# Last eight tiles of the second linear layer: all products copied out of PSUM by ScalarE, all residuals added by TensorE, and a new order table

## The chip, the core and the metric

The kernel runs on one core of a Trainium2 chip. A core has a matrix engine (TensorE, PE in the profile; its weight loads are PEld), a vector engine (VectorE, DVE), an engine for functions of one operand (ScalarE, ACT), a general engine (GpSimd, POOL) and SyncE (SP), whose queue issues nearly all transfers (DMA). Each engine runs its own list of instructions in order and waits on semaphores. Matrix products are written to PSUM, an on-chip memory of accumulators, and have to be read from there by VectorE or ScalarE. SBUF is the on-chip memory of the operands. The metric is device microseconds (us) of one execution; less is better.

## The reference, cut to what matters

There are 2048 tokens of 512 channels and four residual layers, A, B, A, B:

```python
x = x + _A_ref(_layernorm(x), ...)      # memory-augmented attention, 32 heads of 16, 4 segments of 512 tokens
x = x + _B_ref(_layernorm(x), ...)      # linear attention with a learned feature map
x = x + _A_ref(_layernorm(x), ...)      # the same weights again
x = x + _B_ref(_layernorm(x), ...)
```

Layer B is the one that the change touches:

```python
phi_q = concat([softmax(pq), softmax(-pq)])          # 32 features per head and token
phi_k = concat([softmax(pk), softmax(-pk)])
kv  = einsum('bhsf,bhsd->bhfd', phi_k, v);  z = einsum('bhsf->bhf', phi_k)
num = einsum('bhqf,bhfd->bhqd', phi_q, kv)           # the numerators
den = einsum('bhqf,bhf->bhq', phi_q, z) + 1e-06
return (num / den) @ wo                              # then added to x
```

`kv` and `z` sum over all tokens. So no query of a B layer can be finished before the last key of it has been seen, and in the second B layer nothing but its queries is left to do after that.

## The kernel before, in words

The tokens lie in SBUF as 16 tiles of 128 tokens, `X[:, t, :]`. The host code builds a graph of operations for both layer pairs (L = 0 and L = 1): `ln` normalises a tile and transposes it, `a_proj` makes queries, keys and values of a segment of four tiles, `a_att` does the attention of two tiles, `out_proj` multiplies by the output weights and adds the result to `X`, `b_keys` does the key side of B, and `b_query` the query side for a block `c` of four tiles, 4c to 4c+3.

The order of the work is not written in the loops. `ORDER` is a packed table with three parts: the order of all operations, the engine of each (some may run on either ScalarE or VectorE), and the buffer of each tile of the pools. `place` reads it, and `emit` writes each engine's list and the semaphore waits that the data and the reuse of buffers ask for. An operation that takes a buffer waits for all readers of the buffer's last content. PSUM has four such buffers, `pD0` to `pD3`, of 1024 columns each; the pool `p1` of small SBUF tiles has ten, `p2` of larger ones twenty-two. A wait at the head of an engine's list holds up everything behind it on that engine, and SP's queue is such a list too.

The start. The tokens and all weights are loaded by large transfers (512 KB for four tiles of tokens or for one weight matrix), most of them on SP's queue. Tiles 0 to 3 are transposed on PE, and tiles 4 to 7, the second segment, by SP: `xn` (line 597, VectorE) writes a normalised tile and a DMA transpose (line 364) puts it into a buffer of `pX`. The first projection of the second segment needs all four of these transposes. The large loads and the transposes share the queue, so a load that SP issues first is ahead of the transpose.

The end. After the last keys, `b_query` runs for the four blocks of L = 1, in the order 0, 2, 1, 3. For each block, PE makes the query features and their sums (`Zq`), ScalarE takes the exponentials, and a short chain of small ScalarE (`zln`) and VectorE (`zs`) steps makes the 64 weights `AB` per token; line 360 or 359 first copies the sums out of PSUM in blocks 1, 2 and 3 (`Zev`). Then for each tile:

- PE writes the numerators, 128 x 1024 in f32, to a PSUM buffer (`N`).
- They are multiplied by the weights. For a tile in `COPIED`, ScalarE copies them to SBUF as bf16 (`Nev`, line 351) and VectorE multiplies in SBUF (line 1084). For another tile VectorE multiplies straight from PSUM (line 1087).
- VectorE adds the two halves (`nadd`, line 1090). For tiles 0 and 15 PE does it (line 894), and the sum is copied out of PSUM (`ote`).
- SP transposes the result (`otr`, line 364). PE multiplies by the output weights (line 341), for two tiles at a time, and for tiles 14 and 15 one at a time.
- The residual: for tiles in `RES_PE`, PE adds `X` as one more product with the identity matrix, and the sum is copied to `X` by ScalarE (line 359) or VectorE (line 360). For the others, VectorE adds the PSUM buffer to `X` (line 925).
- SP stores the rows of `X` (line 368).

The two branches for the numerators are these:

```python
if (L, t) in COPIED:
    self.act(lambda Ns=Ns: Ns.t[:], lambda N=N: N.t[:], ACT.Copy, 1024, [N], [Ns], label="Nev")
    v(lambda e, ...: e.tensor_tensor(shape(Tm.t[:]), shape(Ns.t[:]), w(), ALU.mult), 600, ...)
else:
    v(lambda e, ...: e.tensor_tensor(shape(Tm.t[:]), shape(N.t[:]), w(), ALU.mult), 1131, ...)
```

Of the kernel before, what the change touches and what calls it, by code (L numbers as in the profile page):

```python
# [297 lines left out]
class Kernel:  # L298
# [147 lines left out]
    def T(self, pool, cls):  # L446
        return Tile(pool, cls)
# [726 lines left out]
c-rlH1GHt=vUXwmSZ&+3ZQHhO+qP}nM$$~$HiJge2)fh%+WRDV$-T+D_l@zt@ngKT_gQnzxvFYbeO2>YYmR-ALkdU(bs;q*fqGCM8bCv61dX8yG=*l+99lq2Xa%jI4  # L1174
YY-J&>lKKN9Y8dp$l|{_>chNK|)9h3KBs|NCpU1p)3F}RD+^W4vK*T0s$IgKx~i@1d$L37OF#Wr~xIQJmiI%kPq@h0jK~ap%#>af>03(K_#dSb)XxRhVD=X3PWZ19;
!eO=n1``2#kbuFbYOPdYA^|U;^}prO*dPz#DiA26Dk2$O)<7G2DfBkQTmy_wX(J08ii^+=r)-9iBlBcmXfr0gQzVkQ*k#c*qLRVGMi)51}u-f&w@gmqC9R0Lx($yoM
oI5C_3F7>*-wJB-B5PzXoi8YqlgU=s9$fv^LHz)BblA@Cz~#p%!yyJ07s0b5}*{DP}tEzE>Zm=VHZD0~fJ@CZWTJJ<=k;ByFu0LXz^@F!RTIWa3{!=GU&YRrzqushC
!9%yh51n~!$4XYqAWCM%Eu^8sTT$m4YV^7SBQy@R~!jJF^Oobvi7KcG+EQ;fBK74}VumDQnI+z83nV=-@h9tNLRzOnhi+dp%B6dNC<FOx3z~nd@*I)`9gKKdWPR0Q^
1?R#-U|bJ`De)UzjU#9gOvK*UA4gIjTnyi0W+;tia07gY-{VG@gzIoWl*a=w2-jl;+<*g7^9uwz2!?;aH~11QBfZ6`m<OieaUeq8h&8bm#>J{w4a;IVjEC{@M-0F$@
CuKCz&bbsD`7>PiPf<(*1#$ljKiol*2Q|b1w-&NI0>n-6xK)L2ABYc(^lMuoA4Zj;yXMKU%+<Uj7#tg%%U$L63@a<_%nXMKum-QF@pC&I39u%FdZAB#E;0d6lc>;+=  # L1180
cUS2QI=!I3E||9Gr`daRDyGCK!eh7=%sH@oRjKvv4=g#%WZTmSII&i7T)ORiYWR95d2%nn`nLE@h$sPK<jn2JXdRZibnuIkv!-7|E^i2(-ZvW^Rj7+zv<4XevwjC_j
~>0u)A@s32{o;uKDWs67^?Q&55g6{9FTM2AVzX^5bhs4xOzLMq&ct*`?s+Cckp5N)K&RE5e@NjiX$RDl9$FvY?%co0uuAjP1Q_!)kVhwv~4Q4BtUr*Ive#ZnXpW8-=
{hhu0geSzty8l|VIG>%GB8OlJRd=v#&ry4Y#T2d>@fXyi*wxBdPfhJN~JcgMtiX^AQwlsv=QB#^iQ)wtQqq<a&CR2TCO>L+F)uzVOgw{|UYDn{_5ly1Clo`)sdaOx?
j)JByu|0L5j&vH2V<5+cT9lPK(R{j&3uqB7p&NJsFXAO!NQ>zv-p1s#ly=ZEN<rIbIqjsBbQm1PBuim@3-90xT1hdvGaaEWbQibNQCdY^DVS#S9KMVr`3inUqj(E_P
O)eo#ina`72{BRN<?v~8}*^S6a`u6B7{&Z4rj&paVs65{j`Vn(lI(n$7wg6pa(dbAL2>6hhum;pQY1Og3r({n!zQx9G{}cn2^fzBTP-_C;^?Pew3XnaSkrVmAN>_=A
j&ib8=$pPCckU^`s;em*dfD8pbm@5vQVAT!AZcVt$Upc?5rj@i_^np|3F+SLbSc8In>c72%>>maFnaeu4*i5?A3e{1nG?DK5>2cmk)TUi1ZhNzbqb51^Xdo7QtKUdS
7G5%1^xe1HpZZXU~Xc`8riaa@q+aUssb11T9@g2J4Tlkx?c!bkZSFXknDkuFg@zDc*J887F_JfEBMU~a%GcmX%$AzY8^^D<t`OSu(i;C0-Z5AzYO#VdIgU#8W3g%WT
b&d8fN6W8VYw1pdUBW}ShxeY&{w%ml<aZ_&3pL0r1#hLjbo#MyTNHi9==_*~LJ9L+>Qx;CnDYyf7<W8KLbJ0o8O?fCi-++z$8E2#Hw3RQwJ*v(5xHISFSg?j~&?deK
X*nzBphxtC&hl|S#|^|bKEVw|7v9NTc{}gor?i82b189}&+uLj5c{~acus+$f~Y9=a5<5a(s4HK#(nubf5H8@KM&wE{3Uni9^8|A@mCZfz9uWmi)R!moQM)J#6ZqV-
_W<zn_p0v2p2Eu6@`d6B2;K$#4Q*mVu{!ySOkff;yW5H>WB+Gi2LwucujG|_Y_ZD<hr7sxWvswebHQ8<|}-QuW~g(qJ@y+4Y8;$9&jb`kcDU|DvP(IL=(|QT!U*IUt  # L1190
EXVe4X#`UB1UPMGetblo5~k9W@nC_&rq-Wkpr-1C0`+MQhPX)Do>kVo_T><)7$BYA4!@&LW9ODw2s`D4|FsK2d4`e1jiz8j)UP5XnVKkxKkbX~hTXA~J~-BBMwrGK(
zYBV`rYM0Sxt+~=E|Lv$76#1;6O$BPM~hj_+c@kG&6Jm+utD)bRAd4%XIMv52wEx+P!qPr*|a*AFemw3&+#rIrNbP%~k9+6iR5^p%4$S(?r!s0tFB8rM)Vvv|Bn#g{
lzZfE#$^l}q7$b&?vEnT^lkfQ*H<ts&4?IOo7L&w}{8UU6)5Q!iQ*;z@pr9x&W{GEFwpb$Oh@bdp{=iGcbMcj!E9Qx1V!l`|R)_^+p;#$aiI2QaeB$+DyZD6{iN#{I
SR>Yo4Pui3u~BRmD9(tpVuxrU&xtR@VX<2r5qm^SxkYRh+r&|^SL_$(#ZIwH>=OsXA#qR~7stex;)1v+E{P86vgoKDidM3<ydqAB&&5e`N<0!*#WnGnxFhb0)8d}EE
^de?@}_toZj1ZkmguB9tH<JN@j`qno``S6OYus)7T<~Q#T(H^eiTn-TiIT=lRt=GL<jjy{wO-ix1y7LC!WjB^1b*Zy2!8O*HX$h3S?XLja0I${7H0^D1R1Ceh^xID_
_f3@`ZdUhs*9VK=zO$<ae^C43uM}kz*yvAlXiRFRf(RU%rv;)c`qCj*{bKupBRid@DobXgNXllD%c9MAcnc)m3#--Bg&IC@0A{GF--$?_`7=DBsI?GE&BuQ8JB8E0f
3=GO0`_)5`=hrpzFJkO^fnnOvrj8D&c8R1Za}r}|O$Qa{N=GL}pw6U)gmwfrD6$=Gs`{8?s}ALVovtg^^KDyy8K2CIUyiYz3v$q<!W7M6WvZ`D_>lmUv>FEW?>Bv;8
m)ko!&*<}v7TCS0cWM37kgjy@B%E7Xq93t<l1bV0pQ;TIkHB45M4^%?^wW=;N=^FC3`bK5e{nZ^cKoya9)jd^I7L%ZYlvGRPQn^g7lQrcOIa^MZbL3n(P0o|k<#IVt
<&}A42{~VulIvwHSzCsyr)s!TDxKD9gi5cUsfu#EnxIz58FGP~DUF(`O3LDLq?)BhsWNh*oFyyC%JPMZr@vJZD!zWMzEY7Yk$$8K>zC@WdZnJIhbpnoprcei8AH8R-
>JQ_h|Z`>>U}ba&ZSG~q&m0WAY-cia-y1~hNz(`g-)sC=#4V2F0QZ3Ec%8lp|k2MvbHWQ>*)AuliVzC%48~=zACTD{IY<YtVXM0>U(ut&Q@FHHhD`<QQ37eom_91Q&  # L1200
nDFN9NHvbSj-jr`2_3PJKYWQ>pcPHBD`iWo0>8PbOD8Wm=U^tyKxsFY1#Tqh9K<iu5bZI=}uw<<mRlI8{KeQw8;p>WzA<=BVm=u98~l8X7d}pVjyJC-qU4)=F#rLCs
UUWO|iBB~*#jdX+-OQYqC2HD7I1TU176bSh<aY_&|y({FScJzt-fWpz1SUVkBr>I%A;J|g3&#44_;FO#S*<srFMZByG-O<hYLl^0}1U0E;Em2_3TSXa}_)dICpEmFt
iXEL?gp$^JSYLmJocgsD}>7*)+DlaR@%qpHLqyzK<9jF)T&*dFiMX%C#WsqL1?#b19jb5vl>ScPlUZI!hx_YBtsT=AIdc9t!>*@Nsk#3+*%M&tEpOib*ad}EEQJeH;
eOKSpP4sQuKsMG5Wix$WH`T#9N*|VuWQdM$n(G!iRL9UU^$N98h3UpJmOdjd%F8lb-_do{1D(LU*N=5w^+f-mU+XODJN;I_(^*wLl}*jmv-E8JRL{``)lEHD-_p-?Z
uPT%t_!J{=7au9$1?TRL)}0XR(aJHokO+M=j3J;q0h?LdX;LZ9_erN11Zfz`9goKizsCt$vo=5T&?n{oa#p%*L>8i^iMjTiEUczIHs5?s@muRs*&2N^Q!<8Xg=w0^)
3zOfY#<0y<7Lx2emOr^ikbQ_tu?t7u{B)X{WpDZo0khpvmM?9d&lqT_4hibzfao9oN;=F?~XB(<k)~-A7kf{q%OdQ#Vn2^$OEe?a?dEe!Wj8HO<r@o!Ioyo%Cn=bIs
<Iek_ZtnyRrnt#_$4YN_h4lNoD*%wRoGCo#chfOck>PG}OD;ktwhGb41k8KrBeA$q7Tsgj!%CennMk-C&RqgR=;I@IhitIbXmWn!47rkP1)mYI|$!n8G`^*McBmsMZ
r)FzE7qe`o^X1Ten+MDL)ifU)Z=oY4<>0rj{PUf0gVy>&DrktvvuByxWhN`8m=-TRmX=6H@)~2!PYPy*&=74!<nwZ_{pxI;gnmwwOS!Y_BL#n(=XN1|Sx|<$mz1d|B
tNx~**=+`x`evMNVA7j==Dt~Ej;Mp`kU4BJn8hZeIiM=49A=+6X119v=D0ay_M7eItQoHxnxkfonV^rVwWg8DWG3pIW|FR?zSI}=MV;AfFdNM|v&n2VL(O?J%p5Vj&
# [61 lines left out]
```

## Time and profile before

| | |
|---|---|
| median of 3 runs | 477.54 us (476.16 to 478.46) |
| the profiled execution, its own time | 477.2 us |
| its span, first to last instruction | 475.5 us |
| PE busy | 450.5 us (95%) |
| ACT busy | 424.1 us (89%) |
| DVE busy | 418.5 us (88%) |
| POOL busy | 54.7 us (12%) |
| granted TensorE clock, mean | 0.996 |

The profile has a page (busy time by engine, the span in 40 slices of 11.9 us, the chain of work that ended last, groups of like instructions) and views of the trace behind it: the timeline of one engine, the chain in order of time, busy time by windows, and the transfers of a window with the time from issue to landing. In a timeline a row gives start, duration, engine, line, operation, tiles, and in brackets the idle time before it with what seems to have ended it. The duration of a row includes its start-up, which overlaps the end of the row before it: from one start to the next on a busy engine, a row costs some 0.1 us less than its duration.

### The profile page before, as it was taken

To read this page: it belongs to the slowest core of one execution; us is meant where nothing else is said; L and a number is where in the kernel's file an instruction comes from. 1 tells how busy PE (TensorE), PEld (TensorE's weight loads), DVE (VectorE), ACT (ScalarE), POOL (GpSimd) and SP (SyncE) were. 2 spreads that over 40 slices of the span, in tenths; PEclk is the share of its full clock that TensorE was granted. 3 is DMA by queue.
4 is the path that set the end of the run, shared out by engine and by line. 5 is a ranking of instruction groups with operands and counts; after the bars stand their busy time and mean duration, and the time that the engine had idled before them with its cause. 6 is when DMAs were issued, how large, how long until landed. Compare 5 with 4: busy or idle time off the path is not lost.

```text
span 475.5 us, 25072 instructions
## 1 busy us (share of the span) xinstructions
PE 450.5 (95%) x11583; PEld 296.2 (62%) x11583; DVE 418.5 (88%) x812; ACT 424.1 (89%) x567; POOL 54.7 (12%) x139
## 2 busy tenths in 40 slices
PE   9979999999999999999999999999999999999885
PEld 4447665767667676565555666666666667666542
DVE  6969999999699888987999998998897887898994
ACT  3869999999999998579999999999999999786961
POOL 2301112001011101100220041110020020110000
PEclk9989999999999999999999999999999999999999
DMA  9941292352423132100133334343104404100256
GB/s 233 248 84 39 42 127 56 76 66 48 69 51 60 25 42 33 24 1 4 37 80 70 81 47 72 69 71 59 26 5 81 61 4 70 37 12 3 55 81 204
DMA packets 89388, 30.36 MB, mean 64 GB/s; under 512 B 75954, under 2 KB 89282, under 8 KB 89282
## 3 DMA queue, kind: packets, MB, share of 16 engines
q1 hardware_dynamic: 88450, 28.20, 32.0%
q8 instruction: 91, 1.49, 1.3%
q10 hardware_dynamic: 800, 0.52, 0.4%
q14 instruction: 15, 0.12, 0.1%
q0 software_dynamic: 32, 0.02, 0.0%
HBM read 6.31 MB, written 2.10 MB: 18 GB/s over the span
## 4 chain that ended last, share of the span: by engine, by line
PE 64%; ACT 21%; DVE 12%; issue 2%; POOL 1%; DVEq 0%
PE D L341 40%; PE D L326 21%; ACT p L351 10%; ACT pF L351 7%; ACT pE L351 3%; DVE p L1087 2%; PE D L662 2%; DVE p L1084 2%; DVE X L925 1%; DVE p L360 1%; DVE p L1090 1%; DVE pT L1007 1%; DVE pK L360 1%; PE D L378 1%; DVE pV L360 1%
## 5 line engine op out<-in xcount | busy, mean ns | idle before, releaser
L351 ACT ACTIVATE p<-D 128x1024 bf16<-128x1024 f32 (+1 forms) x220 | 217.5, 1018 | 12.8 <-PE D L341 7.8
L351 ACT ACTIVATE pF<-D 128x896 bf16<-128x896 f32 x128 | 115.7, 927 | 5.1 <-PE D L326 4.5
L326 PE MATMUL D<-pK,pQ 64*128 64x256 bf16 (+3 forms) x1536 | 113.7, 243 | 4.3 <-ACT pF L351 1.9
L326 PEld LDWEIGHTS D<-pK,pQ 64*128 64x128 bf16 x1536 | 55.4, 94 | 40.8 <-ACT p L351 5.2
L326 PE MATMUL D<-pV,pF 64*128 64x34 bf16 x1024 | 76.5, 176 | 1.6 <-issue 0.8
L326 PE MATMUL D<-pW,pF 64*128 64x34 bf16 x1024 | 73.9, 176 | 0.0
L326 PEld LDWEIGHTS D<-pV,pF 64*128 64x128 bf16 x1024 | 57.2, 93 | 5.8 <-ACT pF L351 2.1
L588 POOL TENSOR_SCALAR rstd<-mv 128x1 f32<-128x1 f32 x60 | 15.0, 256 | 359.7 <-DVE mv L581 359.5
L326 PEld LDWEIGHTS D<-pW,pF 64*128 64x128 bf16 x1024 | 53.5, 93 | 1.4
L326 PE MATMUL D<-pV,p 64*128 64x34 bf16 x1024 | 53.1, 176 | 0.6 <-issue 0.2
L351 ACT ACTIVATE pE<-D 128x768 bf16<-128x768 f32 x64 | 52.1, 821 | 1.5 <-PE D L326 0.9
L326 PE MATMUL D<-pW,p 64*128 64x34 bf16 x1024 | 51.7, 176 | 0.0
L326 PEld LDWEIGHTS D<-pV,p 64*128 64x128 bf16 x1024 | 47.0, 93 | 3.3 <-issue 0.7
L326 PEld LDWEIGHTS D<-pW,p 64*128 64x128 bf16 x1024 | 45.4, 93 | 1.6
L326 PE MATMUL D<-tri,two 64*128 64x128 bf16 (+1 forms) x384 | 46.2, 234 | 0.2 <-issue 0.2
L326 PE MATMUL D<-pV,pE 64*128 64x34 bf16 x512 | 45.0, 175 | 0.0
L580 DVE BATCH_NORM_STATS2 stats<-X 128x6 f32<-128x512 bf16 x64 | 43.2, 682 | 2.0 <-DMA X<-in_A_x_dram 1.7
L326 PE MATMUL D<-pW,pE 64*128 64x34 bf16 x512 | 43.2, 175 | 0.3 <-issue 0.3
L341 PE MATMUL D<-pX,WA_k 64*128 64x512 bf16 x256 | 37.3, 383 | 2.8 <-ACT pF L351 2.6
L972 DVE TENSOR_REDUCE pS<-p 128x64 f32<-128x1024 bf16 (+1 forms) x36 | 38.5, 1090 | 1.4 <-ACT p L351 1.2
L925 DVE TENSOR_TENSOR X<-X,D 128x1024 bf16<-128x1024 bf16 (+1 forms) x29 | 32.0, 1107 | 8.4 <-PE D L341 8.3
L341 PE MATMUL D<-pX,WA_q 64*128 64x512 bf16 x256 | 37.6, 384 | 0.6 <-DVE pV L360 0.5
(132 smaller groups left out, 992.3 us busy)
## 6 DMA issues: line engine op xcount, KB each, us to landing
pW<-pV SPq DMA_DIRECT2D x16, 136.0 KB, 3.6
out_dram<-X SPq DMA_DIRECT2D x7, 256.0 KB, 4.2
X<-in_A_x_dram SPq DMA_DIRECT2D x3, 512.0 KB, 5.7
pX<-in_B_wqkv_dram SPq DMA_DIRECT2D x3, 512.0 KB, 5.0
p<-p SPq DMA_TRANSPOSE x76, 2.7
pX<-p SPq DMA_TRANSPOSE x54, 3.3
WA_k<-in_A_wk_dram SPq DMA_DIRECT2D x2, 256.0 KB, 6.8
WB_o<-in_B_wo_dram SPq DMA_DIRECT2D x8, 64.0 KB, 3.6
```

Source lines behind the costliest of these rows:

```text
L326: ins = e.matmul(out_ap, lhsT, rhs, start=st, stop=sp, tile_position=(basep(lhsT), basep(out_ap)))
L341: ins = e.matmul(out_ap, lhsT[64 * hf:64 * hf + 64], rhs[64 * hf:64 * hf + 64], start=k == 0 and i == 0, stop=k == 1 and i == len(lists[hf ...
L351: return self.g.op({"act": (dur, lambda e: e.activation(out_ap(), in_ap(), func, scale=scale))}, reads, writes, opens, label=label)
L360: "dve": ((340 if fast else n / 0.96 + 65), lambda e: e.tensor_copy(out_ap(), in_ap()))}
L378: ins = e.transpose(pb()[:, k * 128:(k + 1) * 128], src()[:, k * 128:(k + 1) * 128], self.ident[:])
L580: v(lambda e: e.bn_stats(self.stats[:, t, :], self.X[:, t, :]), 602, [R("X", t)], [R("st", t)], label="bn")
L588: v(lambda e: e.tensor_scalar(rs, self.mv[:, t, 1:2], LN_EPS, None, op0=ALU.add), 170, [R("mv", t)], [R("rstd", t)], eng="pool", label="rstd")
L662: ins = e.matmul(D.t[c0:, r0 * 8:r0 * 8 + n], r[:, c0:], ones(r, n), start=True, stop=True, tile_position=(r0, c0))
L925: self.v(lambda e: e.tensor_tensor(X(), X(), src(), ALU.add), 65 + 512 * n / 0.96, pr + xr, xr, label="res")
L972: fn = lambda e, sgn=sgn, eo=eo, Z=Z, n=n: e.tensor_reduce(Z.t[:, 0:64 * n].rearrange("p (k s h) -> p k s h", k=n, s=2)[:, :, sgn, :], eo( ...
L1084: v(lambda e, Ns=Ns, Tm=Tm, w=w, shape=shape: e.tensor_tensor(shape(Tm.t[:]), shape(Ns.t[:]), w(), ALU.mult), 600, [Ns, AB[0], AB[1]], [Tm ...
L1087: v(lambda e, N=N, Tm=Tm, w=w, shape=shape: e.tensor_tensor(shape(Tm.t[:]), shape(N.t[:]), w(), ALU.mult), 1131, [N, AB[0], AB[1]], [Tm], ...
```

## The change

Two sets grow and the table is replaced:

```diff
-RES_PE = {(0, t) for t in (2, 3, 6, 7)} | {(1, t) for t in (2, 3, 6, 7, 10, 11, 14, 15)}
+RES_PE = {(0, t) for t in (2, 3, 6, 7)} | {(1, t) for t in (2, 3, 6, 7, 8, 9, 10, 11, 12, 13, 14, 15)}
-COPIED = {(0, t) for t in range(16)} | {(1, t) for t in range(1, 16, 2)}
+COPIED = {(0, t) for t in range(16)} | {(1, t) for t in range(1, 16, 2)} | {(1, t) for t in range(8, 16)}
 ORDER = """
-c-rlH1GHt=vUXwmSZ&+3ZQHhO+qP}nM$$~$HiJge2)fh%+WRDV$-T+D_l@zt@ngKT_gQnzxvFYbeO2>YYmR-ALkdU(bs;q*fqGCM8bCv61dX8yG=*l+99lq2Xa%jI4
...
+c-rlH1(Y2}vSmPWGl`j*nVFfHnVFfHnVFfH8Ei4wV%Y*)GDx;q*01+ko^N|*c4qhNKMUtqt1GMWMMg&4xN*CxTME)ZU8o23p#e06Mi3toKtf0YNue<`f#eVmQb1E^2
...
```

In L = 1, tiles 8, 10, 12 and 14 go over to the copied branch (four more ScalarE copies, and four multiplies that read SBUF in place of four that read PSUM), and the pairs (8, 9) and (12, 13) over to the residual on PE (eight more matrix products with the identity, and two copies to `X` in place of two additions).

The new table has 2761 operations where the old had 2757. It gives another order, other buffers, and another engine to 21 of the operations that can run on either. Those of them that bear on a count are, in the order of the work:

- at the start, the normalisation `xn` of tile 3 goes from VectorE to ScalarE, and one copy of a weight matrix (`perm`, 512 columns) from VectorE to ScalarE
- in the third and fourth segment of L = 0 two projection copies of 1024 columns change places, one to each engine
- in L = 1 a projection copy of 512 columns goes to VectorE and a copy of 272 columns to ScalarE
- at the end, the copy of the sums of block 1 (`Zev`) and the copy after the addition on PE of tile 0 (`ote`) go from ScalarE to VectorE; the residual copies of tile 14 and of (6, 7) go to VectorE, and those of tile 15, (8, 9) and (12, 13) are on ScalarE

In SP's list at the start, the old table has, after the loads of the first weights, this order: tokens 8 to 11, transpose of tile 7, tokens 12 to 15, transpose of tile 5, weights for B's keys, transpose of tile 4, weights for B's values, transpose of tile 6. The new one has: tokens 8 to 11, tokens 12 to 15, transposes of tiles 6 and 7, weights for B's keys, transposes of tiles 5 and 4, the two swaps of the values (line 736), weights for B's values. Ahead of these stand the same first loads in both; in the new table the A values' weights have moved up, ahead of the second half of the A queries' weights and of the A output weights. In VectorE's list `xn` of tile 6, the last of the four in the old order, comes first, and that of tile 4 last.

At the end, the old list of SP has all stores behind all transposes; the new one has the store of (2, 3) between the transposes of tiles 8 and 4. Four of the additions `nadd` wait in the new table for a transpose as well, the last reader of the `p1` buffer that they write (tile 9 for the transpose of 2, tile 4 for 10, tile 6 for 9, tile 13 for 4).

More of the change, by code (lines that the diff above doesn't have):

```diff
@@ L1178 @@
[L1178 to L1189, printed above, removed]
@@ new lines @@
+O|&C=G?72t0?E@GabdAK*v$1%86NkO+Q;N01ACg;$UR?!jYt0@<Mq^n_lJ4o1Q#NDrf78uW%fkQ44hZWsq+;5Cee4Dbf}!UPx(BVZ{M!UDJq2IC+oj0JHBZiA6H3b#
+X6=nn(oDLjDh;2}(cA+QPh!EzW317HWNhKaBOhT|F-ft#T#Zh>yt5j){@$bmB;C(eX*uoYgwTX=yhVF|2)p)d==;CuK6e#2}q8Fs=h2!+#d0#3n6$c9<)9c0I>I27M
+QcN~U2P~$3Gjq||Z2Y7}V!D4aDjm0n*=EJ<0ABRC6oB}<uC>FstI2@+JY(VUVC2%g3#E$^@2|i(8OoC&vACAM_Fdp|nQXGwIVJ|FzWH=u(K>+>+$#DWY9D|)P1+KxA
+_!8H{LYM<@u?w!n0XTvt;w0>i8=yaqq&~P2O5-9}hY`FO%HVpOjQe2&PQe4P5zFI19E26HEGC9P3}R%$gTR;;p5s)Uh6di@FZe6ILV=ninb@%9AJFl81VW19AF(FJ#
@@ new lines @@
+d25+tKtldht)7X9*4{@6DwjRtd2FX4%Wsh7>skU9@fQ8SQ!)GTnxblxEU8>eI#mtOK=-TKrp1nFQ60#L0m|M3SXndh8T(;FdWapdH52R;&z;e^YIJ}qYH2rV&Fvx!e
+EZTERYC)!bm&>VYmgS<3}%*pK&-X!{s=OcHlJHinD1tHNsig7@J^1oQ;ccCyt`sxC<-NVjN8?u`tb`6<CRi&`iomb0`zdrKZ>n6XQN;jx8{R_uyV^iLJ2>W~O|Up9)
+YI6{NCMh@!9@6{T?6M8#+`2|7fFiMcI?atv;V?J<I4Vid(fNs9JiOlXB2Fb>AX;<O(JQ3;Bq4Rio2(_lJ?0UVP9+0r3Aftq5_VcbXoREA1Zc`8Zga2-{l3UnSz(HN>
+m>nR;orS$X#j-?COoLW$II)X>B24$d=cnSp{!<uv&$I*C7gDt5QWx%vJfimJmN{5*+h|b_qa1_RpGvk+N=pweIA=HlQ(iECXL#ZA$rDiml>Qe)nM2)F7wWc-HhU(Bf
@@ L1233 @@
+qk=hB1SLIh)=N1SkjL4pIrNPA7;1cnGt&5S}v9O>&Tk8R}Z83^?f@cPGS3h{}iCpcjqVXY@ao~Y7)0Ay;S$N
 """
```

96 lines of the change are left out of this document (50 added, 46 removed).

## The prediction

> **What bounds the kernel now.** First the busy shares on the page, by slice.
>
> ```profile
> PE   9979999999999999999999999999999999999885
> DVE  6969999999699888987999998998897887898994
> ACT  3869999999999998579999999999999999786961
> PEclk9989999999999999999999999999999999999999
> ```
>
> One slice is 11.9 us. From the fifth to the 37th PE hardly rests, and ACT only in slices 16 and 17, so time can be won only where all three engines rest at once: in the third slice, where the granted clock falls too, and in the last four. Next, PE's timeline and the windows around the third slice:
>
> ```profile
> 23.52 0.22 PE L326 MATMUL D<-tri,two 64*128 64x128 bf16 x2
> 26.39 1.04 PE L341 MATMUL D<-pX,WA_k 64*128 64x512 bf16 x8 [2.65 <-ACT pF L351]
> 27.25 0.37 PE L326 MATMUL D<-pK,pQ 64*128 64x256 bf16 x4
> 27.44 0.23 PE L326 MATMUL D<-tri,two 64*128 64x128 bf16 x2
> 27.50 1.70 PE L341 MATMUL D<-pX,WA_k 64*128 64x512 bf16 x8
> ...
> 28.00:29.40 1.40, 1.40 (x11) 0.73 (x9) 0.17 (x1) 0.63 (x1) 0.00 (x0) 0.50 0.60 141
> 29.40:31.00 1.60, 1.60 (x11) 0.71 (x8) 1.60 (x5) 1.34 (x2) 0.00 (x0) 0.50 0.41 82
> ```
>
> PE stands still for 2.65 us before the first projection of the second segment, and then the granted clock (third figure from the end) is 0.50 until 31. The timeline names an ACT row as what ended the gap, but the chain in order of time has
>
> ```profile
> 24.46 0.95 ACT pF L351
> 25.41 0.98 issue
> 26.39 1.04 PE D L341 x8
> ```
>
> ACT had been done for 0.98 us, so it was another wait. The code has it: this projection needs the transposes of tiles 4 to 7. In the transfers of the window 19.6 to 21, the last of these is
>
> ```profile
> pX<-p SPq DMA_TRANSPOSE x1, 6.5
> ```
>
> issued at 19.64, so it lands at 26.14, right before PE goes on. The same view gives 4.3, 5.0 and 4.8 us for the other three, issued at 13.28, 15.65 and 17.77. ACT in turn idles 2.32, 1.03, 0.36 and 0.62 us up to 33.2, 4.3 us in all, waiting for PE.
>
> Last, the end, in VectorE's timeline:
>
> ```profile
> 441.13 1.22 DVE L1087 TENSOR_TENSOR p<-D,pS 128x1024 bf16<-128x1024 f32 x1
> 442.27 0.28 DVE L1059 TENSOR_TENSOR pS<-pS,p 128x128 f32<-128x128 f32 x1
> 442.47 0.42 DVE L1090 TENSOR_TENSOR p<-p 128x512 bf16<-128x512 bf16 x1
> 442.80 0.69 DVE L1084 TENSOR_TENSOR p<-p,pS 128x1024 bf16<-128x1024 bf16 x1
> 443.41 0.28 DVE L1060 TENSOR_TENSOR pS<-pS,p 128x128 f32<-128x128 f32 x1
> ...
> 471.02 1.22 DVE L925 TENSOR_TENSOR X<-X,D 128x1024 bf16<-128x1024 bf16 x1 [3.40 <-PE D L341]
> ```
>
> From 438.83, the first `zs`, to 464.57, the end of tile 12's `nadd`, VectorE goes without a pause: it bounds the end. ACT idles 4.8 us in this stretch (0.41, 0.89, 0.84, 0.76, 1.92). Read the steps from start to start: a multiply from PSUM 1.14, one from SBUF 0.61.
>
> **The change part by part.** The sum is made against the profiled execution, 477.2 us (its span of 475.5 and 1.7 around it); the median of 477.54 is 0.34 above.
>
> *Four multiplies moved to SBUF, 8, 10, 12, 14.* VectorE: 4 x (1.14 - 0.61) = -2.1. The table also gives it block 1's `Zev` (0.63, from 440.17 to 440.80) and tile 0's `ote` (0.33 by another copy of 512 bf16, 34.38 to 34.71): +1.0. So -1.1 up to `nadd` of tile 12. ACT: 4 copies at 0.92 (its 1024-wide rows in the chain), less `Zev` and `ote` (about 0.5 each): +2.7, inside its 4.8 idle. I followed both lists by these steps from 438.83: VectorE finds each copy ready, tile 12's by under 0.2, and ends `nadd` of 12 near 463.3 instead of 464.57. In the list of before, PE's last products begin with tile 15's, which need tile 12's PSUM buffer, freed at 464.11, and PE then runs without a break to 470.98. Freed by ACT's copy, the buffer is there by 462; tile 15's own copy then sets the start, near 463.5.
>
> *Two residual pairs on PE.* For (12, 13), two pairs of identity products, 0.22 each by start to start (447.98 to 448.20): +0.4 on PE, which is the path there. Its copy (1.00, ACT row at 455.26) for the last addition (1.22): -0.2. For (8, 9) the same 0.4 lie in PE's idle time of the end (8.91 of 10 us busy from 450 to 460); without that cover they cost 0.4. The addition of (8, 9), 1.13 on VectorE at 464.49, held up tile 14's product; that goes, since ACT copies it.
>
> End: -1.1 + 0.4 - 0.2 = -0.9. Bounds: -2.3 if the two extra copies on VectorE are hidden (-2.1 - 0.2), and +2.9 if every addition to ACT is on the path (2.7 + 0.4 - 0.2). I take -0.9, since the walk above and the 4.8 of cover speak for VectorE, not ACT, as the bound.
>
> *The waits of `nadd` on transposes.* Tiles 9, 4, 6 and 13 wait for transposes of 2, 10, 9 and 4, issued some 5 us earlier or more in the walk; transposes land 2.7 us after issue by the page. Cost 0. Behind such a wait stand the next multiplies, then tile 12's. If the store of (2, 3), which stands ahead of tile 4's transpose, waits for a late ACT copy, it holds SP's queue: up to 1 us.
>
> *SP's list at the start.* One load of 512 KB less is ahead of the last transpose. In the old list tile 4's transpose had exactly the loads ahead of it that it has in the new one, and landed at 17.77 + 4.8 = 22.6. In the new list VectorE has `xn` of tile 4 done near 18 (13.5 to 18.7 in the old list holds the same kinds of rows, and that of tile 6 starts at 18.31), SP issues it near 19, and it lands between 22.6 and 25.5 (19 + 6.5). ACT's list now holds about 2 us more before the projection (two more exponentials), and its last one ends near 24: 24.2 for the projection instead of 26.39. That is -2.2. PE's gap is then about 1 us in two pieces. If the clock stays at 1.00, the five rows up to the first value products (26.39 to 32.24, 5.85 us) take four projections of 0.87 and four score rows of 0.25, 4.5: -1.3. Start: -3.5. Bounds: -4.3, all of ACT's idle time, and 0, if the landing is as late as before. I take -3.5: the landing is nearest to tile 4's old one. The weights moved in the queue (WA_q behind WA_v) are needed at about 14.3; transfers of this kind took 6.3 to 6.8 us in the table of issues, so some 13: cost 0, or 0.5 if later. `xn` of tile 3 on ACT (0.7) is in ACT's idle time.
>
> *ACT's other additions,* `perm` 0.5, 272 columns 0.35, a projection copy less, 0.5: +0.4, at full price, since ACT is busy 24.4 to 25.0 in windows of 25 us there.
>
> *The rest of the order.* Up to the last queries, each engine's work ahead of the same milestone differs by under 1 us in most cases, so a shift won early is kept: 0. From below -2 (ACT's idle time in the saturated windows is some 4 us), from above +4.
>
> Sum: -3.5 + 0.4 + 0 - 0.9 = -4.0, so 473.2 for such an execution, and 473.6 beside the median.
>
> The 2.65 us gap was followed by 3 us at 0.50. The Trainium skill, "TensorE: Matmul & The Clock Gate", section "HAM oscillation", puts the bad gaps above about 3.4 us, an idle window; this gap was shorter. By that rule the slow stretch need not hang on the gap and could stay: the sum would be -2.7. That is rival 3, which needs only the rows above.
>
> **The rivals.**
>
> 1. *The transpose stays late.* For it: tiles 4 and 5 are now both behind the load, and issued one right after the other. Against it: 0.5 MB less ahead. With a landing at 26.1 the start gives nothing, and 477.54 + 0.4 - 0.9 = 477.0.
>
> 2. *ACT becomes the bound of the end.* For it: a copy and a multiply from SBUF take 0.92 + 0.61 against 1.14, and tile 12's copy is ready by a hair. Against it: the 4.8 us of idle. With half of the upper price, +1.8: 477.54 - 3.5 + 0.4 + 1.8 = 476.2. The Trainium skill, "VectorE: DVE Perf Modes", section "Rules for kernel authors", speaks against the change: copy a product out of PSUM first only where many operations follow, and here one does. The rows agree on the sum of both engines (1.53 against 1.14).
>
> 3. *The clock falls all the same,* after the shorter gap: 473.6 + 1.3 = 474.9.
>
> 4. *Slower: new waits in the full middle.* ACT has no reserve from 50 to 175 and 250 to 400. The window 275 to 300 shows what an order can cost: 1.13 us of ACT idle in 25. If the eleven windows there all were so, 12.4 instead of about 4 now: +8.4, and 482.0. It decides from +4.0; from +6.4 the kernel is slower by over 0.5%. For it: the whole table is new. Against it: the milestones agree.
>
> **How the numbers follow.** Chances: forecast 0.45, rival 1 0.17, rival 2 0.12, rival 3 0.09, rival 4 0.17. A change of 0.5% (2.4 us) is about what can be told from none, so faster is below 475.1 and slower above 479.9. Faster: the forecast and most of rival 3, 0.53. Slower: rival 4, 0.17. Within: 0.30. The forecast alone spans 471.5 to 475.5. The range goes from 471.0 (both ends of start and finish together would give 471.3) to 480.0, past rivals 1, 2 and 3 and into the fourth.
>
> **What would show it.** In the new profile: the first second-segment projection near 24 with no clock below 0.9 around it, ACT without a gap from 16 to 35; L1084 x28 and L1087 x4; VectorE's last `nadd` some 4 us earlier than before from the span's start, and ACT idle under 3 us from the first `zs` on to tile 12's copy. I am wrong if the projection still starts after 26, if ACT's waits in the middle grow by over 3 us, or if VectorE waits for ACT's copies at the end.

## The result, and the profile after

The changed kernel takes 474.47 us (median of 5 runs, 473.82 to 474.99), the kernel before 477.18 in the 5 runs beside them: a ratio of 0.9944, 95% interval 0.9928 to 0.9961, so faster by about half a per cent. Its profiled execution took 474.99 us, with a span of 473.3. In a second series the ratio was 0.9952 (0.9930 to 0.9975).

The busy shares by slice (11.8 us each) of the changed kernel:

```profile
PE   9999889999999999999999999999999989999885
DVE  4999989999689968888999999998897887998992
ACT  4799989999999998589999999999999999687981
PEclk9999999999999999999999999999999999999999
```

The third slice is full on PE and the clock's dip is gone. The first slice has become weaker on DVE, and the last four are no fuller. PE's timeline and the windows at the place of the old stall:

```profile
25.75 0.22 PE L326 MATMUL D<-tri,two 64*128 64x128 bf16 x2
25.80 1.03 PE L341 MATMUL D<-pX,WA_k 64*128 64x512 bf16 x8
26.66 0.38 PE L326 MATMUL D<-pK,pQ 64*128 64x256 bf16 x4
26.89 1.04 PE L341 MATMUL D<-pX,WA_k 64*128 64x512 bf16 x8
...
28.00:29.40 1.40, 1.40 (x20) 0.68 (x16) 1.40 (x4) 1.40 (x2) 0.00 (x0) 1.00 0.85 268
29.40:31.00 1.60, 1.60 (x78) 1.23 (x73) 1.60 (x3) 1.58 (x3) 0.00 (x0) 1.00 0.15 50
```

The first projection of the second segment (25.80) no longer has an idle time in front of it, and the clock is 1.00. The first value products start at 29.95 instead of 32.24. The transfers issued between 12 and 22 us show why; first before, then after (count, and median us from issue to landing):

```profile
pX<-p SPq DMA_TRANSPOSE x4, 4.9
```

```profile
pX<-p SPq DMA_TRANSPOSE x4, 3.6
```

But the projection starts at 25.80, not near 24, with nothing in front of it but work. PE came to this place late. The first row of PE's timeline is its warm-up burst (77 products with a matrix of ones, the same in both tables), before and after:

```profile
1.11 7.42 PE L662 MATMUL D<-onesb 128*128 128x512 bf16 x77 [1.11 <-DVE onesb L521]
```

```profile
1.11 8.92 PE L662 MATMUL D<-onesb 128*128 128x512 bf16 x77 [1.11 <-DVE onesb L521]
```

It took 1.5 us longer, and the first projection of all began at 12.29 instead of 10.62.

At the end, the groups of VectorE's instructions from the first `zs` to the end of tile 12's `nadd`, before (438.83 to 464.57) and after (435.13 to 461.17); count, then busy time, mean ns, idle time in front:

```profile
L1087 DVE TENSOR_TENSOR p<-D,pS 128x1024 bf16<-128x1024 f32 x8 | 9.7, 1218 | 0.0
L1084 DVE TENSOR_TENSOR p<-p,pS 128x1024 bf16<-128x1024 bf16 x8 | 5.4, 684 | 0.0
L360 DVE COPY p<-D 128x512 f32<-128x512 f32 x1 | 0.7, 692 | 0.1
```

```profile
L1084 DVE TENSOR_TENSOR p<-p,pS 128x1024 bf16<-128x1024 bf16 x12 | 8.2, 686 | 0.1
L1087 DVE TENSOR_TENSOR p<-D,pS 128x1024 bf16<-128x1024 f32 x4 | 4.9, 1222 | 0.0
L360 DVE COPY p<-D 128x512 f32<-128x512 f32 x2 | 1.4, 689 | 0.1
L360 DVE CAST p<-D 128x512 bf16<-128x512 f32 x1 | 0.7, 685 | 0.0
```

The multiplies cost 2.0 us less (9.7 + 5.4 against 8.2 + 4.9), the two copies taken over from ACT 1.4 more. With the other rows and the overlaps, VectorE is busy 25.11 us of this stretch instead of 25.34, and idle 0.93 instead of 0.40. So the stretch is 26.04 us long instead of 25.74. The rest of the end, in the chain in order of time:

```profile
461.17 1.14 DVE X L925
462.31 0.03 issue
462.34 4.60 DMA p<-p
466.94 0.05 issue
466.99 1.27 PE D L341 x10
```

The transpose of tile 12 takes 4.60 us from issue to landing, and it is on the chain; before, PE's products covered it. From the end of tile 12's `nadd` to the start of the last residual, 8.43 us pass instead of 6.45 (469.60 - 461.17 against 471.02 - 464.57). Before, PE ran through from 464.26 to 470.98. Now its last run begins later relative to that `nadd` (461.92), because the products of (4, 5) waited for a transpose, and then it waits 0.56 us for tile 12's:

```profile
458.54 2.14 PE L341 MATMUL D<-WB_o,p 64*128 64x512 bf16 x16 [1.16 <-DMA p<-p]
...
466.99 0.39 PE L341 MATMUL D<-X,ident 64*128 64x512 bf16 x2 [0.56 <-DMA p<-p]
```

Three points cut both profiled executions into the same pieces of work, since up to each of them both tables have issued the same operations. Start to the first `zs` of L = 0: 214.1 before, 211.8 after (-2.3). From there to the first `zs` of L = 1: 224.7 and 223.3 (-1.4). From there to the end of the span: 36.7 and 38.2 (+1.5). The change gains at the start and in the middle and loses in the very part that its two named edits are in.

### The profile page after: what moved, and what is told of

The parts are those of the page before. It is cut to its first block, busy times and chain, and to the rows that moved or that the text cites. A ratio compares the mean times of both kernels' runs of the same rounds, so it can differ in the third digit from the quotient of the medians.

```text
span 473.3 us, 25111 instructions
## 1 busy us (share of the span) xinstructions
PE 450.8 (95%) x11591; PEld 296.5 (63%) x11591; DVE 417.2 (88%) x811; ACT 427.5 (90%) x572; POOL 55.1 (12%) x139
## 4 chain that ended last, share of the span: by engine, by line
PE 65%; ACT 15%; DVE 13%; DMA 3%; issue 2%; POOL 2%; SPq 0%; DVEq 0%
PE D L341 41%; PE D L326 22%; ACT p L351 6%; ACT pF L351 5%; DMA p<-p 3%; ACT pE L351 2%; DVE X L925 2%; PE D L662 2%; DVE p L1084 2%; DVE p L1090 1%; DVE pT L1007 1%; DVE pS L972 1%; DVE stats L580 1%; POOL rstd L590 1%; DVE p L360 1%
## 5 line engine op out<-in xcount | busy, mean ns | idle before, releaser
L351 ACT ACTIVATE p<-D 128x1024 bf16<-128x1024 f32 (+1 forms) x224 | 220.9, 1020 | 11.9 <-PE D L341 9.0
L588 POOL TENSOR_SCALAR rstd<-mv 128x1 f32<-128x1 f32 x60 | 16.8, 291 | 355.0 <-DVE mv L581 353.8
L972 DVE TENSOR_REDUCE pS<-p 128x64 f32<-128x1024 bf16 (+1 forms) x36 | 38.8, 1091 | 1.0 <-ACT p L351 0.9
L590 POOL TENSOR_TENSOR rstd<-rstd,mhalf 128x1 f32<-128x1 f32 x60 | 35.6, 602 | 3.5
```

Of the source, the lines that this page charges most:

```text
L351: return self.g.op({"act": (dur, lambda e: e.activation(out_ap(), in_ap(), func, scale=scale))}, reads, writes, opens, label=label)
L588: v(lambda e: e.tensor_scalar(rs, self.mv[:, t, 1:2], LN_EPS, None, op0=ALU.add), 170, [R("mv", t)], [R("rstd", t)], eng="pool", label="rstd")
L590: v(lambda e: e.tensor_tensor(rs, rs, self.mhalf[:], ALU.pow), 540, [R("rstd", t), R("mhalf")], [R("rstd", t)], eng="pool", label="rstd")
L972: fn = lambda e, sgn=sgn, eo=eo, Z=Z, n=n: e.tensor_reduce(Z.t[:, 0:64 * n].rearrange("p (k s h) -> p k s h", k=n, s=2)[:, :, sgn, :], eo( ...
```

## The experiments

At those cuts the two tables can be joined: one table's order and engines up to the cut, the other's behind it, with the buffers of the second renamed to fit. A part of the change can thus be run alone. In the tables below, "to zs 0", "middle" and "end" are the three pieces named above, from the profiled execution, in us. Medians over all runs of the kernel before were 478.2 to 479.2 on these chips. The ratios to it, each with its 95% interval, are what is compared; they are not the quotients of the medians, and two of them that differ by less than some 1.5 us (0.3%) are not told apart by them.

### e1 to e4: where the gain is

| | made of | ratio to before (95%) | to zs 0 | middle | end |
|---|---|---|---|---|---|
| before | | 1 | 214.1 | 224.7 | 36.7 |
| changed | | 0.9944 (0.9928 to 0.9961) | 211.8 | 223.3 | 38.2 |
| e1 | old head, new end | 1.0037 (1.0010 to 1.0064) | 213.3 | 225.3 | 37.7 |
| e2 | new head, old end | 0.9906 (0.9878 to 0.9934) | 211.5 | 224.1 | 36.4 |
| e3 | new first half, old rest | 0.9935 (0.9906 to 0.9964) | 211.8 | 225.2 | 36.5 |
| e4 | before, three loads moved | 0.9964 (0.9943 to 0.9986) | 212.6 | 226.1 | 36.4 |

The edits of e1, e2 and e3 (the cut is the first `zs` of L = 1 in e1 and e2, that of L = 0 in e3):

```diff
 e1   up to the cut: table of before;   behind it: new table, COPIED and RES_PE as changed
 e2   up to the cut: new table;         behind it: table of before, COPIED and RES_PE as before
 e3   up to the cut: new table;         behind it: table of before, COPIED and RES_PE as before
```

e4, in SP's list of the kernel before:

```diff
 transpose of tile 7
-load X, tiles 12 to 15
 transpose of tile 5
-load B's value weights
 transpose of tile 4
-load B's key weights
 transpose of tile 6
+load X, tiles 12 to 15
+load B's value weights
 the two swaps of the values (line 736)
+load B's key weights
```

> The order, engines and buffers of the kernel before up to the first VectorE multiplication of the last query chunk group (the first zs of the second layer pair), and those of the changed kernel from there, with both named edits in. My theory after the two traces: the end lost 1.5 us (first zs to the end of the span 36.67 us before, 38.17 after), so this kernel is slower than the kernel before by 1 to 2 us. Rival, the step of the prediction: the end gains 0.9 us, and the 1.5 us in the trace came from how the stage before it hands over; then it is 0.9 us faster. A third: the end is worth nothing by itself (within 0.5 us).

> The reverse: order, engines and buffers of the changed kernel up to the same first zs, and the end of the kernel before, with neither of the two named edits. My theory: all of the gain lies here, 3.5 to 4.5 us faster than before, and so 1 to 2 us faster than the changed kernel as well. Rival (the prediction's split): 3.1 us faster than before (start -3.5, ACT's additions in the middle +0.4), slower than the changed kernel by 0.9.

> The changed kernel's order up to the first zs of the first layer pair (211.8 us in its trace), the order of the kernel before from there on, neither edit. My theory: the start's gain, 2.3 us in the two traces at that point (214.1 against 211.8), stays: 2 to 4 us faster than before, more than 2.3 where TensorE's early matmuls get fast as soon as they did in the trace of before (at 4 us from the start of the span, not at 7). Rival: the rest of the order gives the start's gain back later; then within 0.5 us of before.

> The kernel before with one edit in SyncE's order: the three loads that stood between the transposes of tiles 4 to 7 (X of tiles 12 to 15, and B's raw value and key weights) go behind the last of them. Theory (the prediction's): the late transposes are what the first projection of the second segment waits for, so that projection starts at about 24 instead of 26.39 and TensorE has no stretch at half the clock: 2 to 3.5 us faster. Rival: ACT's list (softmax exponentials) is what sets the start of that stretch, or the loads moved come late for the folding of B's weights: within 0.5 us of before.

The new end alone makes the kernel slower, by 1.8 us (0.37% of 477.2; by the interval 0.5 to 3.1). The new head without the two edits is faster by 4.5 us, about as much more than the changed kernel as e1 loses. Of the gain, 3.1 us are there with the first half alone (e3). For the middle, e3 to e2 leaves 1.4, and by the ratios alone that is not told from nothing; the traces say it more firmly: 223.3 to 224.5 us in nine of the ten profiled executions with the new middle, 224.7 to 226.1 in all four with the old, 1.3 less on average. (The tenth, e11, has 226.1 because of a stop and a slow clock that are told below.)

Some 1.0 us of this is in ACT's own busy time. Over the whole middle ACT is busy 212.3 to 212.7 us in all ten traces with the new middle, and 213.2 to 213.6 in the four with the old. The list of the change says that a projection copy of 512 columns went to VectorE there; by the traces the copy has 1024 columns. In the middle ACT has two copies of that size in line 359 that write a `p` buffer before and one after, of 1.02 us each, and VectorE has six before and seven after in line 360. The copy of 272 columns that came to ACT takes 0.40. Together that is 0.6 of the 1.0. No run has these two copies alone, so that they are the cause isn't shown.

In the two profiled executions ACT also waits less for PE from 262 to 300 us, before and then after:

```profile
270.63 1.73 ACT L351 ACTIVATE pF<-D 128x896 bf16<-128x896 f32 x2 [0.32 <-PE D L326]
286.59 0.92 ACT L351 ACTIVATE pF<-D 128x896 bf16<-128x896 f32 x1 [0.58 <-PE D L326]
290.21 1.73 ACT L351 ACTIVATE pF<-D 128x896 bf16<-128x896 f32 x2 [0.17 <-PE D L326]
295.67 1.94 ACT L351 ACTIVATE p<-D 128x1024 bf16<-128x1024 f32 x2 [0.39 <-PE D L326]
```

```profile
263.13 0.92 ACT L351 ACTIVATE pF<-D 128x896 bf16<-128x896 f32 x1 [0.16 <-PE D L326]
```

But these waits are not what the new table wins: in e9, which is the changed kernel once more, they are 1.41 us in the same 38, about as much as the 1.46 before.

e4 has 1.7 us of the 3.1 (by its interval 0.7 to 2.7) with nothing but three loads out of the way of the transposes. In its timeline the stall at the projection is gone, and the next thing that is late shows, the swap of the values on SP's queue:

```profile
24.35 1.03 PE L341 MATMUL D<-pX,WA_k 64*128 64x512 bf16 x8
...
29.65 0.18 PE L326 MATMUL D<-pV,pF 64*128 64x34 bf16 x1 [0.98 <-DMA pW<-pV]
```

These traces also settle the late start. e2 has the changed kernel's start, operation by operation, and there the burst took 7.48 us:

```profile
1.11 7.48 PE L662 MATMUL D<-onesb 128*128 128x512 bf16 x77 [1.11 <-DVE onesb L521]
...
24.37 1.03 PE L341 MATMUL D<-pX,WA_k 64*128 64x512 bf16 x8
...
28.52 0.18 PE L326 MATMUL D<-pV,pF 64*128 64x34 bf16 x1
```

With the burst as short as in the profile of before, the projection starts at 24.37 and the value products at 28.52, 3.7 us ahead of before. And e1, with the start of the kernel before and a burst of 8.35 us, waits less for the same transposes, and the clock stays at 1.00:

```profile
26.01 1.04 PE L341 MATMUL D<-pX,WA_k 64*128 64x512 bf16 x8 [1.34 <-ACT pE L351]
```

So the old stall is as long as PE is early: transposes that land near 26 cost 2.65 us and a stretch at half the clock in one execution, 1.34 us and no such stretch in another. The clock fell after the gap of 2.65 us and not after that of 1.34.

### e5 to e8, e10: which edit costs

| | made of | ratio to before (95%) | to zs 0 | middle | end |
|---|---|---|---|---|---|
| e5 | changed, residuals of (8, 9), (12, 13) on VectorE | 0.9944 (0.9924 to 0.9963) | 211.2 | 224.5 | 38.9 |
| e6 | e2 and copies of 8, 10, 12, 14 | 0.9951 (0.9930 to 0.9972) | 211.5 | 224.3 | 39.0 |
| e7 | e2 and residuals of (8, 9), (12, 13) on PE | 0.9897 (0.9870 to 0.9925) | 211.0 | 224.0 | 36.6 |
| e8 | e2 and copies of 12, 14 | 0.9906 (0.9877 to 0.9935) | 211.1 | 223.4 | 36.6 |
| e10 | e2 and copies of 8, 10 | 0.9968 (0.9946 to 0.9990) | 211.6 | 224.0 | 38.8 |

e5, on the changed kernel; VectorE adds (8, 9) right behind tile 12's `nadd`, where the kernel before has its residuals:

```diff
-RES_PE = ... | {(1, t) for t in (2, 3, 6, 7, 8, 9, 10, 11, 12, 13, 14, 15)}
+RES_PE = ... | {(1, t) for t in (2, 3, 6, 7, 10, 11, 14, 15)}
```

e6, on e2; e8 and e10 have only (1, 12), (1, 14) and only (1, 8), (1, 10) of it. Each copy goes into ACT's list right behind its numerator:

```diff
-COPIED = ... | {(1, t) for t in range(1, 16, 2)}
+COPIED = ... | {(1, t) for t in range(1, 16, 2)} | {(1, t) for t in (8, 10, 12, 14)}
```

e7, on e2, with both evictions on ACT:

```diff
-RES_PE = ... | {(1, t) for t in (2, 3, 6, 7, 10, 11, 14, 15)}
+RES_PE = ... | {(1, t) for t in (2, 3, 6, 7, 8, 9, 10, 11, 12, 13, 14, 15)}
```

> The changed kernel with one of its two named edits undone: the residuals of (8, 9) and (12, 13) are added by VectorE again, so eight identity products (64x512) leave TensorE and two ACT copies (1.04 and 1.02 us) become VectorE additions (1.2 us each). Theory: the end of the changed kernel is TensorE's (from Wo of (4, 5), it runs 11 us with two gaps of 0.7 and 0.6 us), and the identity products sit in it: 0.4 to 1.0 us faster than the changed kernel, about 473.7 where the kernel before takes 477.2 (ratio to before near 0.993). Rival: the added VectorE work is what the edit saved, and the end is VectorE's: 1.0 us or more slower than the changed kernel (ratio near 0.997 or above).

> e2 (the changed kernel's head, the end of the kernel before; ratio to before 0.9906) plus one of the two named edits alone: ACT copies the numerators of tiles 8, 10, 12 and 14 as well, each right behind its numerator in ACT's order; nothing else in the end is moved. Four VectorE multiplications shrink from 1.22 to 0.68 us (-2.16 us on VectorE), four copies of 1.02 us go to ACT. Theory: ACT was 95% busy in the first 10 us of the end (9.5 of 10 us), so the copies of 8 and 10 push the next scale's logarithms back and eat what VectorE saves: within 0.7 us of e2. The prediction's step (VectorE is the path of the end, -2.1): 1 to 2 us faster than e2, ratio near 0.987. Rival: the copies make ACT the bound: 1 us or more slower than e2 (0.993 and above).

> e2 plus the other named edit alone: residuals of (8, 9) and (12, 13) through the identity on TensorE, and the two evictions on ACT. Theory: 0.4 us of identity products for (8, 9) is on TensorE's run and 0.4 for (12, 13) at its very end; ACT's copy ends the span 0.2 us sooner than VectorE's addition: 0.3 to 0.8 us slower than e2. Rival: taking 1.2 us off VectorE (the addition for (8, 9)) lets its other residuals come earlier: faster than e2 by up to 0.5.

> e2 plus ACT copies of tiles 12 and 14 only, the two that fall where ACT waits (in the end of the kernel before it idles 0.8 us ahead of tile 13's copy and 1.9 us ahead of tile 15's copy of the transpose). VectorE loses 1.08 us of the stretch that ends with tile 12's addition. Theory: VectorE's last stretch feeds the last transpose, and so 0.5 to 1.0 us faster than e2. Rival: TensorE's run of output products (from 460.3 us in the trace of before) covers tile 12's transpose, so nothing is gained: within 0.3 us of e2.

> e2 plus ACT copies of tiles 8 and 10 only, the half of the edit that e8 left out. Theory: these two are the whole loss of e6, because VectorE's multiplication of tile 8 comes to wait for a copy that stands behind the exponentials in ACT's order (2.25 us in e6's trace): 1.5 to 2.5 us slower than e2, ratio near 0.995. Rival: the loss needs all four copies (ACT as a whole is the bound of the end); then about half of it, 1 us, ratio near 0.993.

The residuals are worth nothing that can be told: e7 is 0.4 us better than e2 by the ratios (its end is 0.2 longer), e5 as good as the changed kernel by the ratios (its end is 0.7 to 1.0 longer in the profile). I had expected the identity products to cost 0.3 to 0.8 us, and that isn't seen. The length of e5's end can't be set against the changed kernel's as it stands, though, since the granted clock fell inside it, as the page of e5 shows:

```profile
PEclk9999999999999999999999999999999999999899
```

It was 0.50 from 441.6 to 445.0. The sixteen products at 441.63 took 3.67 us, those in the same place of the changed kernel 2.14, and tile 12's `nadd` ended 27.2 us behind the first `zs` instead of 26.0. Without these 1.2 us the end would be near 37.7, an estimate, and so no longer than the changed kernel's 37.9 and 38.2.

The copies cost, and my expectation for e6 (within 0.7 us of e2) was far off: 2.1 us by the ratios, 2.6 in the length of the end. All of it comes with tiles 8 and 10 (e10 is slower than e2 by 3.0 us by the ratios, 2.4 in the length of the end), none with 12 and 14 (e8). In e6, VectorE, then ACT, around the copy of tile 8:

```profile
447.07 0.42 DVE L1090 TENSOR_TENSOR p<-p 128x512 bf16<-128x512 bf16 x1
449.73 0.69 DVE L1084 TENSOR_TENSOR p<-p,pS 128x1024 bf16<-128x1024 bf16 x1 [2.25 <-ACT p L351]
```

```profile
445.05 2.85 ACT L351 ACTIVATE p<-D 128x1024 bf16<-128x1024 f32 x3
447.76 0.34 ACT L351 ACTIVATE pS<-pS 128x128 f32<-128x128 f32 x1
447.96 0.62 ACT L359 ACTIVATE p<-D 128x512 bf16<-128x512 f32 x1
448.44 0.35 ACT L351 ACTIVATE pS<-pS 128x128 bf16<-128x128 f32 x1
448.64 2.89 ACT L351 ACTIVATE p<-D 128x1024 bf16<-128x1024 f32 x3
```

ACT has no pause here. The copy of tile 8 is the first of the three rows that begin at 448.64, and VectorE's list stands still until it is there. Over the stretch from the first `zs` to tile 12's `nadd` (435.78 to 463.7), the multiplies from SBUF wait for ACT for 3.7 us, more than the 2.1 that they save:

```profile
L1084 DVE TENSOR_TENSOR p<-p,pS 128x1024 bf16<-128x1024 bf16 x12 | 8.1, 685 | 3.7 <-ACT p L351 3.7
```

e10 shows the same wait of 2.25 us in the same place. For e8, VectorE's saving of 1.08 us is met by a wait of 0.94 for ACT's copies of 15 and 14. The Trainium skill, "VectorE: DVE Perf Modes", section "Rules for kernel authors", has a product copied out of PSUM only where many operations follow; e6 and e10 agree with it here, with one operation behind each copy, and e8 shows that even beside an ACT that has time the copy need not gain.

What the new table did with the copies is visible against e6. It moved `Zev` and `ote` to VectorE to make room on ACT, and put the multiplication of tile 8 behind that of tile 9. That removed the waits, and spent VectorE's saving. Taking the copies out of the changed kernel while keeping its order wasn't tried: that order hands the PSUM buffers of tiles 8, 10, 12 and 14 on before VectorE would have read them. So how its loss of 1.4 us divides between copies and order is open.

### e9, e11, e12: the changed kernel again, and a better end

| | made of | ratio to before (95%) | to zs 0 | middle | end |
|---|---|---|---|---|---|
| e9 | changed | 0.9952 (0.9930 to 0.9975) | 212.5 | 224.3 | 37.9 |
| e11 | e2, residuals redistributed | 0.9896 (0.9864 to 0.9927) | 211.2 | 226.1 | 35.5 |
| e12 | e11, products of (6, 7) earlier | 0.9919 (0.9895 to 0.9943) | 211.8 | 224.0 | 37.3 |

e11, on e2 ((8, 9) copied by ACT, the others added by VectorE, in the order (4, 5), (15), (6, 7), (14)):

```diff
-RES_PE = ... | {(1, t) for t in (2, 3, 6, 7, 10, 11, 14, 15)}
+RES_PE = ... | {(1, t) for t in (2, 3, 8, 9, 10, 11)}
```

e12, on e11:

```diff
 ACT:  ... copy of the residual (8, 9)      moved ahead of the copy of tile 15's transpose
 PE:   transpose of 15
+      products of (6, 7)                   in the PSUM buffer of (8, 9)
       products of 15
-      products of (6, 7)
       products of 14
 DVE:  residuals (4, 5), (6, 7), (15), (14)
```

> The changed kernel itself once more, beside the next three on one chip. Expected: ratio to the kernel before 0.9944 again. Its profiled execution shows whether TensorE's warm-up burst, 8.92 us in the first profile of the changed kernel and between 7.42 and 8.35 us in the others, belongs to the kernel or to the execution: if to the execution, as I think, it is anywhere in 7.4 to 8.9.

> e2 with the residuals of the end's last pairs the other way round: (8, 9), where VectorE is full, through the identity on TensorE with an ACT copy as in e7; (6, 7), (14) and (15), where VectorE has nothing else, added by VectorE, as (12, 13) is; no copies added. Theory: from tile 15's transpose on TensorE the end is TensorE's run of output products, which loses three identity groups (0.4 + 0.2 + 0.2 us) against e2: 0.5 to 0.9 us faster than e2, ratio near 0.989. Rival: the transpose of tile 12 (issue to landing 2.4 to 4.6 us) is no longer covered and is waited for: within 0.3 us of e2.

> e11, and the output products of (6, 7) go ahead of those of tile 15, into the 0.7 to 0.8 us in which TensorE waits for ACT's eviction of tile 15's transpose (for that they take the PSUM buffer of (8, 9), whose eviction goes ahead of that one on ACT). Theory: up to 0.7 us faster than e11, if TensorE's run is still the end. Rival: by then tile 12's transpose is what the last products wait for (it can land no earlier than 2.4 us behind its issue): the same time as e11, and a wait for the transpose in front of the last products.

e9: the burst took 8.97 us, at the end of what I had expected. In the ten other executions with exactly this start it took 7.44 (e7) to 8.92, so its length belongs to the execution.

e11's end is 35.5 us, 0.9 below e2's, as expected. PE's last run, with the identity products of (6, 7), 14 and 15 gone:

```profile
463.00 5.85 PE L341 MATMUL D<-WB_o,p 64*128 64x256 bf16 x64 [0.69 <-ACT p L359]
```

By the ratio the whole gain over e2 is 0.5 us, which is not told from nothing. This execution also lost 2 us in the middle, where its order is e2's: PE waited 1.85 us at 289.2 for a transpose, and then the granted clock was 0.50 from 291.2 to 294.6. The page shows it in the slice that holds them:

```profile
PEclk9999999999999999999999998999999999999999
```

Against the changed kernel on the same chip (e9: median 476.54) it is faster by 2.7 us (473.83).

e12 did what it was meant to on PE: its last run has no gap and starts 25.0 us behind the first `zs` of L = 1, not 25.7. But only 0.3 us of this reached the last residual (31.3 against 31.6 us behind that `zs`), and then the kernel lost 2 us behind it: from the start of the last residual to the end of the span 6.0 us pass, in e11 3.9. SP's queue shows where:

```profile
463.31 7.14 SPq L368 DMA_DIRECT2D out_dram<-X  x9
```

The store of tile 15 is the second in this list, and its residual now comes behind that of (6, 7). SP stood for 1.0 us before it, with seven more stores behind, and the last one was out by 470.45, some 2 us after its residual was done at 468.35. Neither of my two theories was right: the end had become the queue of the stores. An end with that list in the order of the residuals wasn't tried. The best versions here are e11 and e7, about 2.5 us faster than the changed kernel and 5 faster than the one before; e2 and e8 are not told apart from them.

## Why the prediction was right, and where it was not

The predicted time was 473.6, and 474.47 was measured; the gain is 2.7 us, where 4.0 was summed. The start was rightly seen. That the whole sum is close is luck: the middle was forecast 0.4 slower and came out 1.4 faster, the end was forecast 0.9 faster and came out 1.8 slower (by e1 to e3: 3.1 + 1.4 - 1.8 = 2.7). Term by term:

- **The start, -3.5.** Right in mechanism and nearly in size. The projection was put at 24.2 with no clock below 1.00, and the value products 3.5 us earlier. With an equal burst (e2) they are at 24.37 and 3.7 us earlier, and e3 measures 3.1 us for the first half. In the changed kernel's own profile it was 25.80 and -2.3. The 4.5 us for the rows up to the value products were 4.15 in both (the prediction calls them five rows; its timeline has eight). What I hadn't seen is that the old stall, and so the gain, depends on how soon PE gets fast, and differs between executions. Rival 1 (the transpose stays late) is out by the landing times and by e4; rival 3 (the clock falls all the same) by a clock of 1.00 from 24 to 34 us in all eleven profiled executions with the new start.
- **"The weights moved in the queue", "xn of tile 3 on ACT", cost 0.** Nearly so: with a burst that is 0.06 longer the first projection of all is at 10.85 (e2) against 10.62.
- **"ACT's other additions: +0.4" and "the rest of the order: 0".** Wrong in sign for the middle, which gained 1.4 (e3 to e2, and 1.3 by the traces). The step that failed is the size of three copies. I took them at 0.5, 0.35 and -0.5; they are 1.22 (`perm`, on ScalarE at 88 us; 0.62 on VectorE), 0.40 and -1.02, since the copy that leaves ACT has 1024 columns. `perm` lies ahead of the middle, so in the middle ACT loses 0.6 us of work, where I had it lose 0.15. The rest of the gain is open. Rival 4, new waits in the middle, did not come: ACT idles 11.0 to 12.0 us in it with the new order (e11 apart) and 11.4 to 12.6 with the old.
- **"Four multiplies moved to SBUF: -1.1 up to `nadd` of tile 12".** The step that failed most. The multiplies save 2.0 by their durations, but from start to start, which is the price that I used, only 1.5 instead of 2.1: in the new order more of them are followed at once by the addition that reads them, and such a step takes 1.26 instead of 1.14 from PSUM and 0.72 instead of 0.61 from SBUF. The two copies taken over cost 1.2 from start to start (0.60 each), not 1.0: `ote` reads f32 from PSUM, and I had priced it by a copy that reads bf16 (0.33). "VectorE finds each copy ready" failed at the weights of block 3 (0.38 waiting for `zln`) and in small holes, 0.5 in all. So the stretch got 0.3 longer (-1.5 + 1.2 + 0.5, rounded). e6 shows that the cover on ACT, 4.8 us of idle time in this stretch, was not where the copies of 8 and 10 are needed. I had counted it as one sum. In the trace of before one pause of 0.41 lies at 440 and the others from 453 on, and those two copies are wanted by 446.6 and 450, where VectorE multiplies tiles 10 and 8.
- **PE's last products "near 463.5".** Relative to the first `zs` this is 24.7; they came at 26.8 (461.92 - 435.13). The products of (4, 5), ahead of them in PE's list, waited 1.16 us for a transpose (1.34 in e9). I had followed the transposes' waits for their buffers ("cost 0") but not PE's list past a transpose that is late.
- **"Two residual pairs on PE: +0.4 and -0.2".** Within what can be told (e5, e7).
- **The end together:** -0.9 forecast, within bounds of -2.3 to +2.9; measured +1.8 by e1 (0.5 to 3.1), and +1.0 to +1.8 in the traces (37.7, 37.9 and 38.2 us with the new end, 36.4 to 36.7 with the old). The lower bound leaves out the +0.4 of the identity products that the sum has; with it, it is -1.9. Rival 2, that ACT becomes the bound of the end, gave +1.8 for it and was nearer than the forecast. It held in e6. In the changed kernel the order avoids ACT's bound and pays for it on VectorE and in PE's waits.

Of the signs, L1084 x28 and L1087 x4 are there. ACT idles 0.34 us from 16 to 35, where it idled 4.39 before, and 2.85 from the first `zs` to tile 12's copy. The last `nadd` of VectorE is 3.4 us earlier than before, not 4 (461.17 against 464.57), and the projection came at 25.80 and not near 24. One slip in the description of SP's list has no part in the sum: the two weights of B are exchanged there; in the old list the values' weights stand between the transposes of tiles 5 and 4 and the keys' between those of 4 and 6, and in the new one the values' come first. All have the same size.

## What to carry to other kernels

Idle time is a cover only where it falls: before an operation is moved to an engine, look for the pause between the moment its input is there and the moment its result is wanted, not for the sum of pauses in the stage. Where the whole order is new, cut both traces at points where the same work has been done, and price the pieces one by one; here the new end, which holds both named edits, lost 1.8 of the 4.5 us that the reordered start and middle won, and the best kernels have the new order up to the end without the four copies. At the end of a kernel every list that is walked in order (PE's products, SP's transposes, SP's stores) can take over as the bound by an operation that waits in it.

## What the runs showed of the hardware that was not expected

- PE's warm-up burst, the same 77 products, took between 7.42 and 8.97 us in fourteen profiled executions, while the row of the granted clock says 1.00 throughout. Its first 14 products are large. They start every 0.43 us at first, and from a moment that moves from one execution to the next every 0.21: from 3.97 us on in the profile of before, while in that of the changed kernel all 14 are slow (the last starts at 6.63). The trace's own record of the clock begins at 3.85 us in the one and at 6.88 in the other. The Trainium skill, "TensorE: Matmul & The Clock Gate", section "Part 1: The HAM clock gate", says that the window in which the activity is watched doesn't begin with the kernel, and that the same kernel therefore starts with a different number of slow products from run to run. The traces agree, but the switch moves by 3 us here (3.85 to 6.97 in the fourteen), where that section gives half a us to each side.
- A short stop of PE can be followed by 3.4 us at a granted clock of 0.50: after 2.65 us (before), after 1.85 (e11), and after 0.72 and 0.41 with 0.41 of work between them (e5). It need not be: after 1.78 us (e5, at 458.7), after 1.34 (e1) and after the same 0.73 and 0.41 in the changed kernel the clock stayed at 1.00. The Trainium skill, "TensorE: Matmul & The Clock Gate", section "HAM oscillation", puts the limit above about 3.4 us; here shorter stops went before it.
- The last transpose of the changed kernel took 4.60 us from issue to the release of PE, where the median of seven in that window is 2.4. What delayed it isn't known; eight stores of up to 256 KB were issued right behind it.
